# Moving weight loads and old-row loads to other steps in a two-attention kernel

## The chip, the cores and the metric

The kernel runs on one core of one Trainium2 chip. The metric is the device time of one execution in microseconds; lower is better. Most executions of a kernel agree within 0.3%.

The core has five engines that run at the same time and wait for one another through semaphores. TensorE (PE in the profile) multiplies matrices, VectorE (DVE) and ScalarE (ACT) work elementwise and reduce, GpSimd (POOL) does elementwise work too, and SyncE (SP) issues nearly all DMA transfers. Every engine works through its own instructions in order. An instruction that waits therefore holds up all that stands behind it on that engine, SyncE's transfers included.

## The reference, cut to what matters

Two attention layers on separate inputs, each with S = 2048 positions, D = 576 columns and 32 heads of 18 columns; the outputs stand side by side.

- A: every position attends to eight positions, its own and those 2, 4, ... 14 before it.
- B: full attention, every position to all 2048.

```
qkv = x @ wqkv                      # both layers
A:  logits = q . k[pos - 2*i], i = 0..7, masked below 0;  softmax over i;  o = sum of attn * v
B:  p = softmax(q k^T / sqrt(18));  o = p v
out = concat(oA @ woA, oB @ woB)    # [1, 2048, 1152], float32
```

## The kernel before

**Order.** The program is written out by hand, step by step. After the projections there are 512 steps: 8 groups of 4 heads of B, and in each group 4 blocks of 512 queries times 16 tiles of 128 keys. Group g begins at step 64 g, so the last group (7) begins at step 448, and its block b at 448 + 16 b. A step issues four score matmuls (line 269), their four exponentials on ScalarE (line 277), and the products of an earlier step with v into the tile `po` (line 742). Everything else is hung between the steps by an agenda: `plan(start, [(n, f), ...])` puts the function f on step start + n, `later(n, f)` puts it n steps after the present one, and `due()` runs what stands on the present step, in the order in which it was put there. What is planned at the start of the program thus stands ahead of what a `later` adds to the same step. The order within the agenda is the order on SyncE's queue and on GpSimd.

**Maxima of B.** The scores are exponentiated after a maximum per query has been taken out. Beside the scores of the present block, TensorE computes scores once more with queries and keys swapped (line 158) and VectorE reduces them (line 166). When all of a block's maxima are there, `least` (line 176) gathers them, `turn` (183) transposes them a step later, `halve` (101 and 102, on GpSimd) splits them into a high and a low half, and `place` (195) writes these as extra rows into the query tile `qs` by eight small DMAs, two steps later in the last group. The first score matmul of a block (line 269) needs these rows. At some steps `together` runs two steps as one, with half an output product of A (line 1245) between their scores.

**Attention A** is computed on GpSimd and VectorE in eight pieces (`local(j)`), each spread over some 80 steps: `match` (914, 918, 921), the softmax (932, 938, 941, 948, 951), `weighted` (957 to 960), the split (964, 969), then a store to `dao` (972), a load of it by heads (`get`, 987 and 989, tiles `at`, `ahl` and for the last half piece `aq`), and the product with woA (1245).

**Output of B.** `finish` normalises a block: it sends the sums out and back through `drec` (785, 787, 788), multiplies on GpSimd (789), splits (790, 791) and stores to `do` (777, or 780 in the last group). The product with woB runs in the last group. Rows of the heads 0 to 27, called old rows, come back from `do` by `fetch_old(b)` (line 1057): four chunks of 126 rows (seven heads), each as a high and a low tile, thus eight DMAs of 252 KB for each block b. They land for b = 0 in the `qs` of group 6's set, for b = 1 in its `ks`, for b = 2 and 3 in other tiles. The rows of the last four heads come by `stack_new` (1076, 1080).

**Weights of B.** `load_wo` loads woB in five chunks: four of 126 rows, the fifth of four pieces of 18 rows. The landing tile `y` is one of four that rotate, shared with output tiles. The fifth chunk's tile is first filled with zeros on GpSimd (854); then come its four DMAs (857), and six steps later the split (101, 102) into the set that group 5 left. `load_wo_stack(p)`, for p = 0 and 1, loads weights for the last four heads in the same manner (877, two DMAs at 879, split), and nine steps later copies the middle rows from lo to hi by two DMAs (886). Before, each chunk of woB stood two steps behind the last from step 455 on, the fifth at 463, the stacks at 465 and 467.

Of the kernel before, what the change touches and what calls it, by code (L numbers as in the profile page):

```python
# [17 lines left out]
D = 576  # L18
H = 32
DH = 18  # L20
# [12 lines left out]
STEPS = NB * NT  # L33
# [15 lines left out]
def ap(t, *dims):  # L49

    return bass.AP(tensor=t.tensor, offset=t.offset, ap=[list(t.ap[0])] + [list(d) for d in dims])


def rows(t, *dims):

    return bass.AP(tensor=t.tensor, offset=t.offset, ap=[list(d) for d in dims])
# [3 lines left out]
def two_attentions(ctx: ExitStack, tc, xa, wa, woa, xb, wb, wob, out):  # L60
# [6 lines left out]
    load = nc.sync.dma_start  # L67
# [32 lines left out]
    def split_on(engine, hi, lo, raw):  # L100
        engine.tensor_copy(hi, raw)
        engine.tensor_sub(lo, raw, hi)
# [5 lines left out]
    def later(n, f):  # L108
        agenda[step + n].append(f)

    def plan(start, pieces):
        for n, f in pieces:
            agenda[start + n].append(f)
# [194 lines left out]
    def halves(r, odd, w, x, wcols, xcols, weights_move=False):  # L308

        at = slice(64 * r, 64 * r + 64)  # L310
        both = [p for c in range(4) for p in pairs(c, w, x, wcols, xcols)] + pairs(4, w, x, wcols, xcols)[: 1 + (r == odd)]
        return [(b[at], a[at]) if weights_move else (a[at], b[at]) for a, b in both]
# [68 lines left out]
    with (tc.tile_pool(name="x", bufs=1, side="right") as xp,  # L381
# [103 lines left out]
        if True:  # L485
# [9 lines left out]
            chunks = [[(0, 0, 128)], [(0, 128, third - 128), (D, 0, 256 - third)], [(D, 256 - third, 128)]]  # L495
# [185 lines left out]
            for k in range(2, 14):  # L681
                n = 46 if k == 2 else 36 + 4 * k
# [7 lines left out]
            def leave_a(c, b, n, ps):  # L690
                o = xp.tile([128, 512], F32, name="ohi", bufs=4)
                nc.scalar.activation(o[:n], ps, AF.Copy)  # L692
                load(da[128 * c : 128 * c + n, HALO + 512 * b : HALO + 512 * b + 512], o[:n])
# [23 lines left out]
            for c, b in order:  # L717
                n = min(128, 3 * D - 128 * c)
                work_list.append(((b % 2, ws[c][0], xas[b][0], slice(0, n), every),
                                  lambda ps, n=n: ps[:n], lambda ps, c=c, b=b, n=n: leave_a(c, b, n, ps)))  # L720
# [123 lines left out]
    wo = {}  # L844
# [1 line left out]
    producing = set()  # L846
    copied = set()

    def load_wo(k, src, *pieces):

        raw = work.tile([128, D], F32, name="y", bufs=4)
        n = 0
        if len(pieces) == 4:
            nc.gpsimd.memset(raw, 0.0)
            n = 128
        for at, c0, m in pieces:
            load(raw[at : at + m], src[c0 : c0 + m])
            n = max(n, at + m)
        if k == "a":
            hi = work.tile([128, D], F32R, name="wohi", bufs=5)  # L860
            lo = work.tile([128, D], F32R, name="wolo", bufs=5)
        else:

            c = len(wo.get(k, []))
            hi, lo = (ap(t[:, 0, 0, :] if len(t.shape) == 4 else t[:, 0, :], (1, NB * 1024))[:, D * c : D * c + D]
                      for t in sets[(NG - 3) % 3])
        wo.setdefault(k, []).append((hi, lo))
        later(3 if k == "a" else 6, lambda: split_on(nc.gpsimd, hi[:n], lo[:n], raw[:n]))

    wstack = []  # L870
# [1 line left out]
    def load_wo_stack(p):  # L872

        hi, lo = (ap(t[:, 0, 0, :] if len(t.shape) == 4 else t[:, 0, :], (1, NB * 1024))[:, D * (5 + p) : D * (6 + p)]
                  for t in sets[(NG - 3) % 3])
        raw = work.tile([128, D], F32, name="y", bufs=4)
        nc.gpsimd.memset(raw, 0.0)
        for r in range(2):
            load(raw[64 * r : 64 * r + 3 * DH], rows(wob[DH * (H - 4 + r + 2 * p)], (0, 3), (D, DH), (1, D)))
        wstack.append(hi)  # L880
        later(6, lambda: split_on(nc.gpsimd, hi[:118], lo[:118], raw[:118]))

        def middle():
            for r in range(2):
                at = slice(64 * r + DH, 64 * r + 2 * DH)
                load(hi.bitcast(F32)[at], lo.bitcast(F32)[at])

        later(9, middle)


    def local(j):
# [104 lines left out]
            for_two.add(inside[-1])  # L996

        def sums_of_a(h, n, alone=True):
            his, los = zip(*wo["a"])
            w = his[:4], los[:4], his[4], los[4]  # L1000
            cols = slice(288 * h, 288 * h + 288)
            if h == 0:
                st["y"] = ys["a", j, n] = work.tile([128, D], F32, name="y", bufs=4)
            y = st["y"][:, cols]
            both = [halves(r, 0, w, st["x", n], cols, slice(0, 128), True) for r in range(2)]
            if not alone:
                return both, y
            one, two = beside("scores", *both)
            nc.scalar.activation(y, two, AF.Copy)
            behind_scores.append(lambda: nc.vector.tensor_add(y, one, y))  # L1010
# [3 lines left out]
        pieces = [(33, lower), (35, exponents), (39, share), (60, upper), (61, rest), (64, lambda: put(0)), (66, lambda: put(1))]  # L1014
# [5 lines left out]
        pieces = [(at - soon, f) for at, f in pieces]  # L1020
# [14 lines left out]

    olds = defaultdict(list)

    def fetch_old(b):
        for c in range(4):
            h, n = 7 * c, 126  # L1040
            if b < 2:

                t = sets[(NG - 2) % 3][b]
                o = ap(t[:, c, 0] if b == 0 else t[:, c // 2, 1024 * (c % 2) :], (512, 2), (1, 512))
                o = o[:, 0], o[:, 1]

            elif b == 2:
                o = [work.tile([128, D], F32R, name=nm, bufs=5)[:, :512] for nm in ("wohi", "wolo")]
            elif c < 2:
                o = work.tile([128, 2, 512], F32R, name="pr", bufs=2)  # L1050
                o = o[:, 0], o[:, 1]
            else:
                o = ap(work.tile([128, DH, HALO + SUB], F32R, name="akv", bufs=2), (512, 2), (1, 512))
                o = o[:, 0], o[:, 1]
            for i in range(2):
                first = do[i, h // 4, 32 * (h % 4), 512 * b : 512 * b + 512]
                load(o[i].bitcast(F32)[:n], rows(first, (32 * S, 7), (S, DH), (1, 512)))
            olds[b].append([t[:n] for t in o])
# [47 lines left out]
    def beside(kind, *both):  # L1106

        sums_ = [bank(k)[:, :288] for k in (kind, None)]
        turns = [[(sums_[r], *ab, i == 0, i == len(t) - 1) for i, ab in enumerate(t)] for r, t in enumerate(both)]
        pair = kind and sum(given) + 2 <= NG * NB * PIECES * 2  # L1110
        if pair:

            for r in range(2):
                turns[r].insert(6 + 4 * r, None)
        for i in range(max(map(len, turns))):
            for r in range(2):
                if i < len(turns[r]):
                    if turns[r][i]:
                        ps, a, b, start, stop = turns[r][i]
                        nc.tensor.matmul(ps, a, b, start=start, stop=stop)  # L1120
                    else:
                        maximum(r)()
        if pair:

            rings["else"].append(rings["else"].pop(0))
        return sums_
# [72 lines left out]
    for k, src, start, chunks in (  # L1199
        ("a", woa, 28, [[(0, 128 * c, 128)] for c in range(4)] + [[(64 * r, 512, 64) for r in range(2)]]),  # L1200
        ("b", wob, STEPS * (NG - 1) + 7,
         [[(0, 126 * c, 126)] for c in range(4)] + [[(32 * i, 504 + DH * i, DH) for i in range(4)]]),
    ):
        plan(start, [((4 if k == "a" else 2) * c, lambda k=k, src=src, ch=ch: load_wo(k, src, *ch)) for c, ch in enumerate(chunks)])
    for j in range(NJ):
        plan(AT[j], local(j))
    for g in range(1, NG):
        if g > EARLY:
            plan(STEPS * (g - 2) + 1, [(n, f) for n, f in enumerate(stack_loads(g))])
        if g == NG - 1:  # L1210
            plan(STEPS * g, [(4, lambda: fetch_old(0)), (17, lambda: load_wo_stack(0)), (19, lambda: load_wo_stack(1)),
                             (24, lambda: fetch_old(1)), (34, lambda: fetch_old(3)),
                             (38, lambda: fetch_old(2))])
            plan(STEPS * g, [(n, lambda t=t, h=h: partial(t, h)) for n, (t, h) in
                             zip((43, 44, 45, 47, 49, 51), [(t, h) for t in range(3) for h in range(2)])])
            plan(STEPS * g, [(62, lambda: outside.append(lambda: first(3, NB - 1, 0)))])
            for b in range(NB - 1):
                producing.update(STEPS * g + NT * (b + 1) + (23, 15, 7)[b] + n for n in range(8))
        plan(STEPS * (g - 1), [(24, lambda g=g: load_v(g))])
# [52 lines left out]
    while step < ALL:  # L1272
        n, kt = divmod(step, NT)
        g, b = divmod(n, NB)
# [80 lines left out]
```

## Time and profile before

| what | value |
|---|---|
| median of three runs | 1606.92 us (1605.85 to 1607.03) |
| profiled execution | 1605.83 us |
| its span, first to last instruction | 1604.0 us |
| TensorE busy | 1585.2 us, 99% |
| VectorE busy | 1363.6 us, 85% |
| ScalarE busy | 1215.1 us, 76% |
| GpSimd busy | 965.2 us, 60% |
| mean granted clock of TensorE | 0.998 |

The span leaves out what lies before the first and after the last instruction, 1.8 us here. Times in rows of a timeline count from the start of the span. A row of a timeline gives start, length, engine, line, operation, the tile written and the tile read, and in brackets how long the engine was idle before and what ended that. A row of a stretch gives its bounds, its length, the busy time and the number of instructions of each engine, the granted clock, the busy share of the 16 DMA engines, and GB/s. Where rows are merged, "x8" counts instructions. A row of waits gives the engine, the tile and the line that waited, for whom, and then the total, the number and the longest.

### The profile page before, as it was taken

The page shows a single profiled execution, that of the slowest core. Times are in us where ns is not written, and L with a number is a line of the kernel's source. Part 1 is how long each engine was busy: PE and PEld are TensorE (multiplying, and loading weights), DVE is VectorE, ACT ScalarE, POOL GpSimd, SP SyncE. Part 2 cuts the span into 40 slices and gives each one's busy share as a digit, 9 for nine tenths or more (in the row PEclk, how much of TensorE's full clock was granted, in tenths as well). Part 3 has the DMA queues.
Part 4 walks back from the last instruction along what each step waited for, and adds up shares of the span by engine and source line. Part 5 has one row for each costly group of instructions (what it writes and reads, how often), then busy time and mean ns, then how long its engine had stood idle before and what let it go on. Part 6 is the DMA issues. An engine that isn't in the chain of part 4 may idle for free.

```text
span 1604.0 us, 34970 instructions
## 1 busy us (share of the span) xinstructions
PE 1585.2 (99%) x13276; PEld 963.5 (60%) x13276; DVE 1363.6 (85%) x2315; ACT 1215.1 (76%) x2438; POOL 965.2 (60%) x798
## 2 busy tenths in 40 slices
PE   9999999999999999999999999999999999998998
PEld 7999888999543444444445444445445445545676
DVE  5199999999999999999999999999999999896522
ACT  7323441121699999999999999999999999996655
POOL 2305742210266994995896896897896797791000
PEclk9999999999999999999999999999999999999999
DMA  9837954532221362254326335332632231154311
GB/s 264 224 125 196 273 167 130 146 105 80 60 55 50 83 155 67 52 125 96 73 80 146 77 88 119 96 87 54 135 100 66 61 98 36 51 166 153 120 62 60
DMA packets 188025, 175.66 MB, mean 110 GB/s; under 512 B 119416, under 2 KB 133240, under 8 KB 186128
## 3 DMA queue, kind: packets, MB, share of 16 engines
q1 hardware_dynamic: 182992, 161.88, 36.7%
q0 software_dynamic: 4032, 10.63, 3.1%
q8 instruction: 104, 1.70, 0.5%
q10 hardware_dynamic: 832, 0.92, 0.2%
q14 instruction: 65, 0.53, 0.1%
HBM read 98.77 MB, written 73.47 MB: 107 GB/s over the span
## 4 chain that ended last, share of the span: by engine, by line
PE 91%; DVE 3%; DMA 2%; ACT 2%; POOL 1%; issue 1%; SPq 0%; POOLq 0%; DVEq 0%
PE po L742 28%; PE bank L269 18%; PE bank L158 17%; PE bank L364 16%; PE bank L301 5%; PE bank L1120 4%; PE bank L1245 3%; DVE mx L166 3%; ACT e L277 1%; DMA den<-o 1%; DMA rec<-drec 1%; POOL xlo L412 1%; PE bank L516 0%; ACT lg L941 0%; DMA out<-y 0%
## 5 line engine op out<-in xcount | busy, mean ns | idle before, releaser
L166 DVE TENSOR_REDUCE mx<-bank 128x2 f32<-128x512 f32 x2048 | 1279.8, 683 | 132.8 <-PE bank L158 100.2
L277 ACT ACTIVATE e<-bank 128x512 f32<-128x512 f32 x2048 | 1047.5, 607 | 72.6 <-PE bank L269 66.4
L158 PE MATMUL bank<-ks,qs 54*128 54x512 f32 (+1 forms) x2466 | 791.7, 382 | 4.5 <-DVE mx L166 3.0
L158 PEld LDWEIGHTS bank<-ks,qs 54*128 54x128 f32 x2466 | 404.5, 184 | 387.8 <-DVE mx L166 339.4
L269 PE MATMUL bank<-qs,ks 56*128 56x512 f32 x2048 | 597.4, 426 | 6.6 <-DMA qs<-mt 6.6
L742 PE MATMUL po<-e,v 128*19 128x512 f32 x4096 | 531.4, 598 | 0.0
L269 PEld LDWEIGHTS bank<-qs,ks 56*128 56x128 f32 x2048 | 309.7, 185 | 37.8 <-ACT e L277 24.6
L914 POOL TENSOR_TENSOR pr<-aq,akv 128x1024 f32<-128x1024 f32 x72 | 158.4, 2201 | 15.7 <-DMA akv<-da 12.9
L957 POOL TENSOR_TENSOR pr<-lg,akv 128x1024 f32<-128x1024 f32 x72 | 158.4, 2200 | 0.6
L742 PEld LDWEIGHTS po<-e,v 128*19 128x19 f32 x4096 | 73.8, 97 | 138.4 <-issue 132.9
L918 POOL TENSOR_TENSOR pr<-pr 128x1024 f32<-128x1024 f32 x64 | 152.5, 2383 | 5.0
L692 ACT ACTIVATE ohi<-bank 128x512 f32<-128x512 f32 (+1 forms) x56 | 30.4, 595 | 149.2 <-issue 98.5
L364 PE MATMUL bank<-xhi,ahi 64*128 64x512 f32 (+1 forms) x448 | 114.4, 387 | 0.0
L364 PE MATMUL bank<-xhi,alo 64*128 64x512 f32 (+1 forms) x448 | 110.5, 387 | 0.0
L364 PE MATMUL bank<-xlo,ahi 64*128 64x512 f32 (+1 forms) x448 | 107.7, 388 | 0.1
L1245 PE MATMUL bank<-wohi,at 64*128 64x288 f32 x480 | 103.5, 305 | 0.0
L958 POOL TENSOR_TENSOR pr<-pr 128x512 f32<-128x512 f32 x72 | 92.5, 1284 | 5.6
L1245 PEld LDWEIGHTS bank<-wohi,at 64*128 64x128 f32 x480 | 74.7, 184 | 27.6 <-ACT e L277 23.8
L412 POOL TENSOR_TENSOR alo<-raw,ahi 128x512 fp32r<-128x512 f32 (+1 forms) x14 | 17.5, 1253 | 121.0 <-ACT ahi L411 99.4
L504 POOL TENSOR_TENSOR olo<-olo,ohi 128x512 fp32r<-128x512 f32 x36 | 46.0, 1292 | 61.3 <-ACT ohi L503 55.5
L1245 PE MATMUL bank<-wolo,at 64*128 64x288 f32 x240 | 70.0, 292 | 0.0
L364 PEld LDWEIGHTS bank<-xhi,ahi 64*128 64x128 f32 (+1 forms) x448 | 64.6, 182 | 3.5
(202 smaller groups left out, 1793.9 us busy)
## 6 DMA issues: line engine op xcount, KB each, us to landing
do<-n SPq DMA_DIRECT2D x30, 512.0 KB
da<-ohi SPq DMA_DIRECT2D x52, 256.0 KB
akv<-da SPq DMA_DIRECT2D x64, 175.5 KB
out<-y SPq DMA_DIRECT2D x32, 288.0 KB
qs<-dqk SPq DMA_DIRECT2D x30, 288.0 KB
ks<-dqk SPq DMA_DIRECT2D x30, 288.0 KB
at<-dao SPq DMA_DIRECT2D x60, 128.0 KB
rec<-drec SPq DMA_DIRECT2D x29, 256.0 KB
```

The lines of the kernel that those rows point to most:

```text
L158: return nc.tensor.matmul(ps if part is None else ps[:, 256 * r : 256 * r + 256], qs[at, b, p, 128 * t : 128 * t + 128], ks[at, p, 512 * k ...
L166: nc.vector.tensor_reduce(at, ps.rearrange("q (s n) -> q s n", s=2), axis=AX.X, op=ALU.max)
L269: nc.tensor.matmul(ps, ks[at, p, 128 * kt : 128 * kt + 128], qs[at, b, p], start=True, stop=True)
L277: nc.scalar.activation(e, ps, AF.Exp, scale=SCALE)
L301: nc.tensor.matmul(ps, a, b, start=c == i == 0, stop=c == 4 and i == 1)
L364: nc.tensor.matmul(ps, a, b, start=start, stop=stop)
L742: nc.tensor.matmul(po[32 * i : 32 * i + 19], vs[g][:, kt, 19 * i : 19 * i + 19], es[i], start=kt == 0, stop=kt == NT - 1)
L914: nc.gpsimd.tensor_mul(pr, ap(st["q"][:, 2 * c], (SUB, 2), (0, W), (1, SUB)), window(st["k"], c))
L918: nc.gpsimd.tensor_add(st["pr"], st["pr"], pr)
L957: nc.gpsimd.tensor_mul(at, ap(st["lg"], (0, 2), (SUB, W), (1, SUB)), window(st["v"], c))
L958: nc.gpsimd.tensor_add(at[:, :, :4], at[:, :, :4], at[:, :, 4:])
L1245: return nc.tensor.matmul(ps, a, b, start=r == k == 0, stop=r == 1 and k == len(both[1]) - 1)
```

## The change

- The fifth chunk of woB begins at step 421 instead of 463, the stacks at 423 and 425 instead of 465 and 467. All three are thus in group 6.
- Their DMAs are issued three steps after the zero fill instead of right behind it (424, 426 and 428). The split stays six steps after the beginning (427, 429, 431) and the copies of line 886 nine steps after it (432 and 434 instead of 474 and 476).
- Because the fifth chunk now comes ahead of the other four, the chunks of `wo` are kept under their number and no longer as a list in order of loading.
- `fetch_old(1)`, eight DMAs at step 472, becomes two calls of four DMAs: chunks 0 and 1 at step 458, chunks 2 and 3 at step 462.

```diff
-    def load_wo(k, src, *pieces):
+    def load_wo(k, src, c, *pieces):
         raw = work.tile([128, D], F32, name="y", bufs=4)
         n = 0
+        def fetch():
+            for at, c0, m in pieces:
+                load(raw[at : at + m], src[c0 : c0 + m])
         if len(pieces) == 4:
             nc.gpsimd.memset(raw, 0.0)
             n = 128
-        for at, c0, m in pieces:
-            load(raw[at : at + m], src[c0 : c0 + m])
-            n = max(n, at + m)
+            later(3, fetch)
+        else:
+            n = max(at + m for at, c0, m in pieces)
+            fetch()
...
-            c = len(wo.get(k, []))
...
-        wo.setdefault(k, []).append((hi, lo))
+        wo.setdefault(k, {})[c] = hi, lo
...
     def load_wo_stack(p):
...
         nc.gpsimd.memset(raw, 0.0)
+        def fetch(r):
+            load(raw[64 * r : 64 * r + 3 * DH], rows(wob[DH * (H - 4 + r + 2 * p)], (0, 3), (D, DH), (1, D)))
         for r in range(2):
-            load(raw[64 * r : 64 * r + 3 * DH], rows(wob[DH * (H - 4 + r + 2 * p)], (0, 3), (D, DH), (1, D)))
+            later(3, lambda r=r: fetch(r))
...
-    def fetch_old(b):
-        for c in range(4):
+    def fetch_old(b, start=0, end=4):
+        for c in range(start, end):
...
-        plan(start, [((4 if k == "a" else 2) * c, lambda k=k, src=src, ch=ch: load_wo(k, src, *ch)) for c, ch in enumerate(chunks)])
+        plan(start, [((4 if k == "a" else 2) * c if len(ch) < 4 else 421 - start, lambda k=k, src=src, c=c, ch=ch: load_wo(k, src, c, *ch))
+                     for c, ch in enumerate(chunks)])
+    plan(423, [(0, lambda: load_wo_stack(0)), (2, lambda: load_wo_stack(1))])
...
-            plan(STEPS * g, [(4, lambda: fetch_old(0)), (17, lambda: load_wo_stack(0)), (19, lambda: load_wo_stack(1)),
-                             (24, lambda: fetch_old(1)), (34, lambda: fetch_old(3)),
+            plan(STEPS * g, [(4, lambda: fetch_old(0)), (10, lambda: fetch_old(1, 0, 2)), (14, lambda: fetch_old(1, 2, 4)),
+                             (34, lambda: fetch_old(3)),
                              (38, lambda: fetch_old(2))])
```

More of the change, by code (lines that the diff above doesn't have):

```diff
@@ L998, in sums_of_a @@
         def sums_of_a(h, n, alone=True):
-            his, los = zip(*wo["a"])
+            his, los = zip(*(wo["a"][c] for c in range(5)))
             w = his[:4], los[:4], his[4], los[4]
```

## The prediction

> **What bounds the kernel now.** I read the page first (busy time of each engine), then TensorE's list of waits, then stretches of 40 us and of 2 us, then TensorE's and SyncE's timelines around the one wait that is left.
>
> ```profile
> span 1604.0 us, 34970 instructions
> ...
> PE 1585.2 (99%) x13276; PEld 963.5 (60%) x13276; DVE 1363.6 (85%) x2315; ACT 1215.1 (76%) x2438; POOL 965.2 (60%) x798
> ```
>
> TensorE is busy for 1585.2 of 1604.0 us, and the change neither adds, removes nor reorders a matmul. So it can pay, or cost, only in TensorE's waits and in the clock that follows them. From 1270 us to the end its list of waits has one that stands out:
>
> ```profile
> PE bank L269 <- DMA qs<-mt: 6.6, 1, 6.6
> ...
> 1444.00:1484.00 40.00, 33.43 (x294) 21.80 (x292) 27.57 (x48) 25.73 (x52) 5.69 (x7) 0.91 0.43 155
> ...
> 1470.00:1472.00 2.00, 2.00 (x15) 1.95 (x14) 0.90 (x2) 1.49 (x3) 0.00 (x0) 0.50 0.73 250
> ...
> 1474.00:1476.00 2.00, 2.00 (x21) 0.43 (x18) 0.79 (x2) 0.72 (x2) 0.00 (x0) 1.00 0.41 142
> ```
>
> In the rows of stretches the last three columns are granted clock, DMA share and GB/s. The 40 us with the wait hold 33.4 us of matmul, and after the wait the clock is at half speed for some microseconds. What wait and clock cost together is read from one repeated piece of work: two steps with half a product of attention A between them. It begins with a matmul of line 1245 and ends where line 742 begins.
>
> ```profile
> 1455.25 0.40 PE L1245 MATMUL bank<-wohi,at 64*128 64x288 f32 x1
> ...
> 1459.45 1.91 PE L742 MATMUL po<-e,v 128*19 128x512 f32 x16
> 1461.30 0.40 PE L1245 MATMUL bank<-wohi,aq 64*128 64x288 f32 x1
> ...
> 1462.47 0.29 PE L1245 MATMUL bank<-wolo,aq 64*128 64x288 f32 x1
> 1469.33 0.76 PE L269 MATMUL bank<-qs,ks 56*128 56x512 f32 x1 [6.57 <-DMA qs<-mt]
> ...
> 1474.10 1.91 PE L742 MATMUL po<-e,v 128*19 128x512 f32 x16
> ...
> 0.00:1462.80 1462.80, 979.07 (x1918) 1.00 0.42 111
> ```
>
> An undisturbed piece takes 1459.45 - 1455.25 = 4.20 us; this one takes 1474.10 - 1461.30 = 12.80. The excess is 8.6 us: 6.57 of wait and 2.03 of slow clock. The last row counts exponentials of line 277, four to a step: 1918 is two past 4 x 479, so the stall falls inside the pair of steps 479 and 480, at the first scores of step 480 = 448 + 32, block (7, 2). They wait for that block's maxima rows, which place() (line 195) writes into qs.
>
> Why the rows are late stands in SyncE's timeline (start, length, line, DMA, count) and its waits:
>
> ```profile
> 1444.93 6.20 SPq L1057 DMA_DIRECT2D ks<-do  x8
> 1451.24 1.48 SPq L777 DMA_DIRECT2D do<-n  x1
> 1452.77 1.18 SPq L788 DMA_DIRECT2D rec<-drec  x1
> 1454.05 4.77 SPq L886 DMA_DIRECT2D qs<-ks  x4
> 1459.60 6.08 SPq L195 DMA_DIRECT2D qs<-mh  x4
> 1465.78 2.18 SPq L195 DMA_DIRECT2D qs<-mt  x4
> ...
> SPq L195 <- DMA rec<-drec: 2.3, 1, 2.3
> ...
> 1454.86 0.21 POOL L101 CAST mh<-mt 128x32 fp32r<-128x32 f32 x1 [3.29 <-DVE mt L183]
> ...
> 1467.45 1.53 DMA qs<-mt
> ...
> ks<-do SPq DMA_DIRECT2D x8, 252.0 KB
> ```
>
> GpSimd has the rows' high half ready at 1455.07. SyncE is then inside line 886, the four copies of load_wo_stack's middle(), and begins place() only at 1459.60; its first four issues take 6.08 us, because SyncE waits for transfers in flight. Those are the eight old-row loads of block 1 issued from 1444.93 (8 x 252 KB) with the store and the rec load behind them. The chain has the last mt transfer at 1467.45 plus 1.53 us.
>
> **The change part by part.** *Removed around the wait.* Gone from steps 463 to 476 are the loads of the fifth chunk (4 DMAs) and of the two stacks (2 each), the four copies of line 886, and from step 472 the eight ks<-do. At step 474 only the store and the rec load remain; both are then free of the queue that held them. place() would start when GpSimd is ready, at about 1455.1. An undisturbed place is the one of block (7, 1):
>
> ```profile
> 1413.14 0.35 SPq L787 DMA_DIRECT2D drec<-den  x1
> 1416.54 2.36 SPq L195 DMA_DIRECT2D qs<-mh  x4
> 1419.02 2.16 SPq L195 DMA_DIRECT2D qs<-mt  x4
> ...
> 1426.70 0.49 PE L269 MATMUL bank<-qs,ks 56*128 56x512 f32 x1
> ...
> 0.00:1426.90 1426.90, 947.37 (x1856) 1.00 0.42 110
> ```
>
> It issues in 4.64 us (1416.54 to 1421.18). From the end of the last mt issue (1465.78 + 2.18 = 1467.96) to its landing (1468.98) and to TensorE's start (1469.33) were 1.0 and 1.4 us. So the rows are there at 1455.1 + 4.6 + 1.0 to 1.4 = 1460.7 to 1461.1, and TensorE comes at 1462.76 (1469.33 - 6.57): the wait goes to zero with 1.7 us to spare, and the slow clock with it. Ends: a full gain of 8.6; and, if the store and rec still slow the issue by as much as rec did (2.3 us), a wait of 0.6 us and a gain of 8.0. I take 8.6, since their issue no longer follows eight old-row loads.
>
> The Trainium skill's page "TensorE: Matmul & The Clock Gate" (Part 1, the HAM clock gate) says that TensorE falls to half clock after an idle window of about 3.4 us and returns after as much work; this trace agrees: 6.57 us of idle, then 0.50 granted at 1470, 1.00 at 1474. By that rule a leftover wait of 0.6 us would cost no clock.
>
> *Old rows of block 1 in two parts.* Four loads now go out at step 458 and four at 462. The first four stand in the agenda of step 458 ahead of block (7, 1)'s place, since they are planned at the start and place is added later: the same queue, the same neighbour, one block earlier. SyncE has 1413.5 to 1416.5 free for it (drec ends its issue at 1413.49; place waits for GpSimd until 1416.54), and four issues at 6.20 / 8 each are 3.1 us: no delay of the issue, or 0.1. The transfers are 4 x 252 KB = 1.03 MB, and part of what was loaded before is still in flight:
>
> ```profile
> 1413.50:1421.50 8.00, 8.00 (x66) 3.48 (x64) 7.41 (x13) 8.00 (x17) 7.53 (x10) 1.00 0.22 74
> ...
> 1450.00:1452.00 2.00, 2.00 (x24) 1.87 (x21) 2.00 (x4) 2.00 (x4) 1.48 (x2) 1.00 0.45 173
> ```
>
> In the eight microseconds from 1413.5 the trace moves 0.59 MB (74 GB/s). With 1.03 MB more it is 1.62 MB; at the 173 GB/s seen where mostly old rows were moving, that is 9.4 us, done at 1422.9, and mt lands at about 1424, 2.7 us before step 464 (1426.70; the count 1856 = 4 x 464 dates it). Ends: nothing, and 3.7 us if it lands as late after readiness as at step 480 (1468.98 - 1455.07 = 13.9 us; 1416.5 + 13.9 = 1430.4). I take nothing: ahead of it is half of what was ahead there.
>
> The Trainium skill's page "DMA: Bandwidth & Descriptors" (Why a DMA increments its semaphore by 16 and not by 1, on how many engines) says that a DMA runs on the largest count up to 16 that divides the slowest dimension of both sides; seven heads on the DRAM side would give 7 of 16. The DMA share of 0.45 (7.2 of 16) at 1450 agrees. It speaks against the change in one point: splitting the block does not make the old rows faster, and the first half keeps the queue busy for some 6 us (1.03 MB at the row's 173 GB/s), which the sum above already pays.
>
> The second four go out at about 1424.5, behind the first dao store. Behind them are the second dao store and the loads of at and aq for the last products of A, which are pushed back by 1.03 MB and forward by the eight weight loads that have gone, with SyncE's waits on their memsets. The rows are that store, the last of those loads, and the first matmul that takes one:
>
> ```profile
> 1424.06 0.41 SPq L972 DMA_DIRECT2D dao<-aohi  x1
> ...
> 1442.15 0.59 SPq L989 DMA_DIRECT2D aq<-dao  x1
> ...
> 1449.20 0.40 PE L1245 MATMUL bank<-wohi,at 64*128 64x288 f32 x1
> ```
>
> 1.03 MB at 173 GB/s are 6.0 us, the cover is 1449.2 - 1442.7 = 6.5 us, and the first at was issued still earlier: nothing.
>
> *Fifth chunk and stacks at 421 to 434.* GpSimd gets three memsets and three splits there, 3 x 0.58 + 3 x (0.67 + 1.43) = 8.0 us by the rows below, and loses them after 1427:
>
> ```profile
> 1427.83 0.58 POOL L854 MEMSET y<- 128x576 f32 x1
> ...
> 1437.86 0.67 POOL L101 CAST qs<-y 128x576 fp32r<-128x576 f32 x1
> 1438.61 1.43 POOL L102 TENSOR_TENSOR ks<-y,qs 128x576 fp32r<-128x576 f32 x1
> ...
> 1348.94 1.29 POOL L921 TENSOR_TENSOR lg<-pr 128x512 f32<-128x512 f32 x1
> 1355.70 1.29 POOL L938 TENSOR_TENSOR lg<-lg,am 128x512 f32<-128x512 f32 x1 [5.48 <-DVE am L932]
> ...
> 1351.21 0.42 DVE L932 TENSOR_TENSOR am<-lg 128x256 f32<-128x256 f32 x1
> ...
> 1362.51 0.69 ACT L941 ACTIVATE lg<-lg 128x512 f32<-128x512 f32 x1
> ```
>
> Two memsets come ahead of line 921 in program order (steps 421 and 423), so lg ends at 1351.3 instead of 1350.2. VectorE wants it at 1351.21: it would stand 0.1 to 0.3 us. The third memset and two splits, 0.6 + 4.2 us, fill the 5.48 us hole behind line 921; line 938 comes at most 0.5 us later, and ScalarE needs it only at 1362.5. VectorE holds up TensorE's banks when it is late, so I charge 0.2 us, between 0 and 0.5.
>
> The loads there wait on those memsets, so SyncE stands until about 1351.8 at the second stack's. Queued behind it are a rec load and the next at loads; nothing that TensorE takes before step 432. Line 886 moves to 432 and 434, where no maxima rows are due: nothing.
>
> *Sum.* -8.6 + 0.2 = -8.4 us. Against the profiled execution (1605.83 us, span 1604.0) that is 1597.4, span 1595.6. The median of the runs shown, 1606.92, is 1.09 above it: 1598.5.
>
> **Next in line.** After step 480 the old rows of blocks 3 and 2 and the last heads' rows are issued as soon as SyncE is free, so they move forward with TensorE. TensorE's list names no wait there that is set by a transfer.
>
> **The rivals.** (a) *Part of the gain is given back*: rows at step 464, at step 475 or still at 480 land so late that TensorE loses 2 to 5 us. For it: cover of only 2.7 us at 464 and 1.7 us at 480; against: half the bytes ahead. Time 1600.5 to 1603.5. (b) *The change doesn't do what it says*: store, rec load and whatever is delayed from 1424 on still fill the queue at 1451, and place stays as slow. For it: SyncE did wait longest there on the rec load (2.3 us). Against: that load is 256 KB and stood behind 2 MB. Time 1606.9 + 0.2 = 1607.1. (c) *Slower*: the wait goes from step 480 to 464. Were the 1.62 MB to move at the 74 GB/s of 1413.5 to 1421.5, they would take 22 us, mt lands at 1436, TensorE waits 9.3 us and loses 2.03 us of clock: 11.3 - 8.4 = +2.9, time 1609.8. It turns slower from a wait of 6.4 us there (8.4 - 2.03), mt after 1433. Against: 74 GB/s is a queue running empty (share 0.22).
>
> **How the numbers follow.** Forecast 0.70, with its own range 1597.2 to 1600.5 (gain 8.0 to 8.6, VectorE 0 to 0.5, and 1.1 us of scatter: the runs lie between 1605.85 and 1607.03); (a) 0.16; (b) 0.08; (c) 0.06. 0.2% is 3.2 us, about what runs of this kernel can tell from no change: faster is below 1603.7. Faster: 0.70 + 0.15 of (a) = 0.85; same: 0.01 + (b) + 0.01 of (c) = 0.10; slower 0.05. The range 1597.0 to 1604.0 holds the forecast and (a).
>
> **What would show it.** Right: no wait of line 269 on qs<-mt near 1462; granted clock 1.00 all through 1444 to 1484; SyncE at line 195 by 1455.2 with issues of 2.3 and 2.2 us; ks<-do in two groups of four near 1413 and 1424; the hole of 5.48 us ahead of line 938 filled. Wrong: a new wait at 1426.7 (step 464) or at line 1245 near 1449, or the old one kept with a shorter queue ahead of it.

## The result, and the profile after

The changed kernel takes 1605.08 us (median of 22 runs, 1603.06 to 1607.17) against 1606.87 us before (22 runs). The ratio is 0.9989, 95% interval 0.9983 to 0.9996: 1.8 us faster, between 0.6 and 2.7. The prediction was 1598.5 us with a range from 1597.0 to 1604.0.

The profiled execution took 1607.17 us, the longest of the 22; its span is 1605.4 us. It lies 2.8 us behind that of before already at the den load of step 417 (1326.13 instead of 1323.37), ahead of the first step that the change touches (421); why is not known. So absolute times of the two traces differ by about 3 us up to step 470, and only lengths within one trace are compared here.

The wait at step 480 is gone, as predicted, and a new one stands eight steps ahead of it, between steps 471 and 472 (the expectations below call it step 471). The first row of TensorE's waits of the changed kernel from 1270 us on:

```profile
PE bank L158 <- DVE mx L166: 5.6, 3, 5.1
```

and what VectorE waited for, from all engines' waits from 1440 to 1456 us:

```profile
DVE den L786 <- DMA den<-o: 5.2, 1, 5.2
```

The first line 158 matmul of each of the steps 470 to 474, from TensorE's timeline of the changed kernel:

```profile
1442.00 0.38 PE L158 MATMUL bank<-ks,qs 54*128 54x256 f32 x1
...
1444.02 0.38 PE L158 MATMUL bank<-ks,qs 54*128 54x256 f32 x1
...
1451.23 0.58 PE L158 MATMUL bank<-ks,qs 54*128 54x256 f32 x1 [5.08 <-DVE mx L166]
...
1454.86 0.58 PE L158 MATMUL bank<-ks,qs 54*128 54x256 f32 x1
...
1457.42 0.38 PE L158 MATMUL bank<-ks,qs 54*128 54x256 f32 x1
```

and two stretches of it (the last three columns are clock, DMA share, GB/s):

```profile
1452.00:1454.00 2.00, 2.00 (x15) 0.73 (x11) 1.73 (x3) 1.94 (x4) 0.00 (x0) 0.50 0.68 154
...
1458.00:1460.00 2.00, 2.00 (x20) 0.90 (x19) 1.93 (x4) 2.00 (x4) 0.00 (x0) 1.00 0.22 70
```

An undisturbed step takes 1444.02 - 1442.00 = 2.02 us. The three steps from 1444.02 to 1457.42 take 13.40 instead of 6.06: a loss of 7.3 us, 5.1 of wait and 2.2 of slow clock. The old place lost 8.6. The difference, 1.3 us, is most of the measured 1.8.

What VectorE waited for is the den load of block (7, 0), 8 KB, issued by SyncE. SyncE's timeline of the changed kernel:

```profile
1419.51 2.31 SPq L195 DMA_DIRECT2D qs<-mh  x4
1421.93 2.16 SPq L195 DMA_DIRECT2D qs<-mt  x4
1424.13 3.18 SPq L1066 DMA_DIRECT2D ks<-do  x4
1427.35 0.51 SPq L777 DMA_DIRECT2D do<-n  x1
...
1430.60 5.90 SPq L1066 DMA_DIRECT2D ks<-do  x4
1436.74 2.14 SPq L981 DMA_DIRECT2D dao<-ao  x1
1438.99 0.60 SPq L785 DMA_DIRECT2D den<-o  x1
1441.86 3.21 SPq L996 DMA_DIRECT2D at<-dao  x2
...
1465.35 2.29 SPq L195 DMA_DIRECT2D qs<-mh  x4
1467.74 2.15 SPq L195 DMA_DIRECT2D qs<-mt  x4
```

the piece of its chain of waits that is den's way (start, length):

```profile
1438.99 10.70 DMA den<-o
```

and the reciprocal in VectorE's timeline:

```profile
1449.78 0.25 DVE L786 RECIPROCAL den<-den 128x16 f32<-128x16 f32 x1 [5.24 <-DMA den<-o]
```

The same two instructions in the kernel before, in SyncE's and VectorE's timelines:

```profile
1432.85 0.62 SPq L785 DMA_DIRECT2D den<-o  x1
```

```profile
1441.48 0.24 DVE L786 RECIPROCAL den<-den 128x16 f32<-128x16 f32 x1
```

Before, den went out 8.6 us ahead of the reciprocal. The traces also record each count that a transfer adds to its semaphore when it lands; by these counts den landed at 1439.05 then, after 6.2 us, with 2.4 us to spare. Now the second half of the old rows (5.90 us on SyncE for four loads, where the first half took 3.18) and the dao store stand ahead of it. VectorE is ready for the reciprocal at 1449.78 - 5.24 = 1444.54, and den goes out only 5.6 us ahead of that and takes 10.7 us. So it goes out 3.1 us later and is 4.5 us longer on its way; less the 2.4 us of cover, that is the wait of 5.2. By the same counts the old rows ahead of it landed at 1447.95 and the dao store at 1449.44, den at 1449.69.

The 5.90 us are not slower issuing. The four issues by themselves take 3.25 us. The rest is waiting for earlier transfers, mostly the first half of the old rows, as SyncE's waits from 1400 to 1480 us show:

```profile
SPq L1066 <- DMA ks<-do: 2.3, 2, 1.2
```

In these traces eight semaphores take turns among the transfers, and a transfer goes out only when the one eight places ahead of it, which used the same semaphore, has landed: the second, third and fourth load of the second half went out at 1432.52, 1434.75 and 1435.78, each 0.02 us after the last count of its predecessor. So a transfer that is still on its way holds up SyncE eight places later.

The reciprocal is planned on step 470, in VectorE's order ahead of the maxima of the following steps. So VectorE stands for 5.2 us with the reductions behind it, the score banks are not given back, and TensorE stands.

### The profile page after: what moved, and what is told of

Read it like the earlier page. It is cut to its first block, busy times and chain, and to the rows that moved or that the text cites. A ratio compares the mean times of both kernels' runs of the same rounds, so it can differ in the third digit from the quotient of the medians.

```text
span 1605.4 us, 34964 instructions
## 1 busy us (share of the span) xinstructions
PE 1586.9 (99%) x13276; PEld 962.1 (60%) x13276; DVE 1363.3 (85%) x2315; ACT 1214.7 (76%) x2438; POOL 965.1 (60%) x798
## 4 chain that ended last, share of the span: by engine, by line
PE 90%; DVE 4%; DMA 2%; ACT 1%; POOL 1%; issue 0%; SPq 0%; POOLq 0%; DVEq 0%
PE po L742 28%; PE bank L269 18%; PE bank L158 17%; PE bank L364 15%; PE bank L301 5%; PE bank L1256 4%; PE bank L1129 4%; DVE mx L166 3%; DMA den<-o 1%; ACT e L277 1%; POOL xlo L412 1%; DMA dqk<-olo 1%; PE bank L516 0%; DMA more<-xa 0%; DVE as L941 0%
## 5 line engine op out<-in xcount | busy, mean ns | idle before, releaser
L101 POOL CAST mh<-mt 128x32 fp32r<-128x32 f32 x32 | 6.7, 210 | 111.5 <-DVE mt L183 111.5
```

## The experiments

The theory from here on: the change has two parts that work against each other. The early weight loads take away the wait at 480; the early old rows put a new one at 470 to 471, by way of den. The rival: any megabyte that is put ahead of the end of attention A stalls something, so the gain cannot be had. Each comparison is with the kernel before on the same chip.

| run | median us | before us | ratio (95%) | wait of TensorE |
|---|---|---|---|---|
| weights_only | 1600.15 | 1606.65 | 0.9957 (0.9945 to 0.9968) | 480: 0.3 |
| old_only | 1609.75 | 1606.65 | 1.0016 (1.0008 to 1.0025) | 471: 8.9 |
| half_late | 1598.92 | 1606.65 | 0.9953 (0.9941 to 0.9965) | none over 0.6 |
| late_reciprocal | 1599.25 | 1606.65 | 0.9952 (0.9940 to 0.9964) | 480: 0.3 |
| den_on_scalar | 1609.87 | 1607.08 | 1.0016 (1.0007 to 1.0025) | by ScalarE: 8.5 |
| copies_later | 1604.66 | 1607.08 | 0.9985 (0.9976 to 0.9994) | 480: 4.7 |
| loads_early | 1602.50 | 1607.23 | 0.9973 (0.9963 to 0.9984) | 480: 3.0 |

**weights_only: the first part alone.**

```diff
-            (10, lambda: fetch_old(1, 0, 2)), (14, lambda: fetch_old(1, 2, 4)),
+            (24, lambda: fetch_old(1)),
```

> The changed kernel with the old rows of block 1 back at step 472, all eight at once; the weight loads stay early. Theory (the changed kernel lost at step 471 what it won at step 480, because the den load of block (7, 0) sat behind the second half of the old rows): no wait of VectorE for den; at step 480 SyncE reaches line 195 by 1455 instead of 1459.6 (the four copies of line 886, 4.77 us, are gone), its issue still slowed by the eight loads, a wait of 0 to 4 us there; 1599 to 1603 us. Rival (the old rows alone set the wait at 480): it stays at 5 us or more, 1605 to 1607 us.

SyncE's timeline of this run:

```profile
1442.57 6.23 SPq L1066 DMA_DIRECT2D ks<-do  x8
1448.91 0.57 SPq L777 DMA_DIRECT2D do<-n  x1
1449.53 0.66 SPq L788 DMA_DIRECT2D rec<-drec  x1
1455.56 2.28 SPq L195 DMA_DIRECT2D qs<-mh  x4
1457.94 4.23 SPq L195 DMA_DIRECT2D qs<-mt  x4
```

and TensorE's wait at 480:

```profile
PE bank L269 <- DMA qs<-mt: 0.3, 1, 0.3
```

All eight old-row loads stand where they stood before, and the wait is 0.3 us. They are still felt (the mt issue takes 4.23 us instead of 2.15; in SyncE's waits, line 195 stands 2.0 us for the rec load, which went out behind them), but the spare time before step 480 covers all but 0.3 us of that. The second part of the change was not needed for 6.5 us of gain.

**old_only: the second part alone**, in the kernel before.

```diff
-    def fetch_old(b):
-        for c in range(4):
+    def fetch_old(b, start=0, end=4):
+        for c in range(start, end):
...
-            (24, lambda: fetch_old(1)),
+            (10, lambda: fetch_old(1, 0, 2)), (14, lambda: fetch_old(1, 2, 4)),
```

> The kernel before with only the old rows of block 1 moved (458 and 462); the weight loads stay at 463 to 476. Theory: den of block (7, 0) is late by at least as much as in the changed kernel (VectorE waits 5 to 9 us at step 471), and at step 480 a wait of 0 to 2 us is left, since the copies of line 886 still stand ahead of line 195; 1605 to 1610 us. Rival (the early weight loads of group 6 are what costs): no wait at 471, 1598 to 1600 us.

SyncE's timeline of this run:

```profile
1430.55 5.82 SPq L1057 DMA_DIRECT2D ks<-do  x4
1436.54 5.08 SPq L857 DMA_DIRECT2D y<-wob  x4
1442.98 0.36 SPq L972 DMA_DIRECT2D dao<-ao  x1
...
1447.53 0.61 SPq L785 DMA_DIRECT2D den<-o  x1
```

and VectorE's wait:

```profile
DVE den L786 <- DMA den<-o: 9.1, 1, 9.1
```

With the weight loads still between the old rows and den, den goes out at 1447.53 and VectorE waits 9.1 us. At step 480 TensorE does not wait, though the weight loads and the copies of line 886 still stand ahead of line 195; but the stall at 471 has given them 9 us more. Moving the old rows costs more than the wait at 480 that it takes away: 0.16% slower.

**half_late: the second half out of den's way.**

```diff
-            (10, lambda: fetch_old(1, 0, 2)), (14, lambda: fetch_old(1, 2, 4)),
+            (10, lambda: fetch_old(1, 0, 2)), (24, lambda: fetch_old(1, 2, 4)),
```

> The changed kernel with the second half of block 1's old rows at step 472 instead of 462. Theory: den is in time (its load is issued by 1433 and lands within 5 us), and four loads do not delay the maxima rows at 480; no wait over 1 us after 1270 us, 1597 to 1600 us. Rival (whatever 1 MB is put ahead of the end of attention A stalls something): a wait of 3 us or more somewhere between 1440 and 1470, 1602 us or more.

The den load in SyncE's timeline of this run:

```profile
1431.74 0.60 SPq L785 DMA_DIRECT2D den<-o  x1
```

the reciprocal in VectorE's:

```profile
1443.33 0.24 DVE L786 RECIPROCAL den<-den 128x16 f32<-128x16 f32 x1
```

and SyncE's longest wait from 1423 to 1450 us:

```profile
SPq L996 <- DMA dao<-aohi: 9.0, 1, 9.0
```

The reciprocal has no idle time before it, and the gain is 7.7 us. But den did not land within the 5 us that I expected: by its semaphore it landed at 1442.91, 11.2 us after its issue and 0.4 us ahead of the reciprocal. It was in time because it went out early, and only just. The first half still does harm off the path: the loads of at wait 9.0 us for the dao store to land behind it, which is covered.

**late_reciprocal: the den load stays, VectorE comes to it later.** The drec store and the rec load, which follow from the reciprocal, stand three and two steps later too.

```diff
-        times = ... else (1, 6, 7, 10, 13, 14, 15, 16)
+        times = ... else (1, 9, 10, 12, 13, 14, 15, 16)
```

> The changed kernel with no transfer moved, but in the last group VectorE's reciprocal of den three steps later (nine steps behind the block's end instead of six), drec's store ten and the rec load twelve steps behind it. Theory: the wait at step 471 goes, because VectorE then comes to den after it has landed; what is late next are the loads of at, which the changed kernel issued until 1451.1, so at step 475 TensorE waits 0 to 2 us; 1598 to 1601 us. Rival (the load on the queue stalls TensorE anyway, by at): a wait of 4 us or more at step 475, 1603 to 1606 us.

The reciprocal in VectorE's timeline of this run, and the first matmul on at in TensorE's:

```profile
1449.76 0.24 DVE L786 RECIPROCAL den<-den 128x16 f32<-128x16 f32 x1
```

```profile
1451.37 0.40 PE L1256 MATMUL bank<-wohi,at 64*128 64x288 f32 x1
```

The den load is as long on its way as in the changed kernel (issued at 1438.14, landed at 1448.71 by its semaphore, 10.6 us), VectorE takes the reciprocal at the same time (1449.76 here, 1449.78 there), and no wait of TensorE there is over 0.3 us: the place of one small instruction in VectorE's order, with the two transfers that follow from it, decided the loss. The 0 to 2 us that I expected at step 475 for at did not come. The rival falls with this run and half_late.

**den_on_scalar: the den load from another engine.**

```diff
-    lambda: load(den, o[DH:128:32])
+    lambda: (load if g < NG - 1 else nc.scalar.dma_start)(den, o[DH:128:32])
```

> The changed kernel with every transfer at its step, but in the last group the 8 KB den load is issued by ScalarE instead of SyncE. It tells apart two halves of the delay: den was issued at 1438.99 in the changed kernel (six microseconds later than before, SyncE being held at the old rows and the dao store) and landed 10.7 us after that. If the order on SyncE and on its queue is the cause: the load goes out by 1434 and lands in under 5 us, no wait of VectorE for den, TensorE loses at most 2 us at step 475; 1598 to 1601 us. If the transfer engines themselves are taken up by the old rows and the stores, whoever issues: den still lands after 1445, VectorE waits 2 us or more, 1602 to 1605 us.

Neither reading came out: den landed after 1445, as the second had it, but VectorE did not wait for it, and the time is worse than both. (The six microseconds of the expectation compare times of two traces that lie 3 us apart; measured within each trace, as above, it is 3.1.) Two pieces of the chain ("issue" is time in which the engine waited for nothing that the profile shows):

```profile
1431.98 7.51 issue
1439.50 1.14 ACTq L785
```

and TensorE's timeline:

```profile
1440.74 0.58 PE L158 MATMUL bank<-ks,qs 54*128 54x256 f32 x1 [8.49 <-ACTq L249]
```

ScalarE came to the load at 1431.98 and began to issue it at 1439.50. That was not slow issuing but a wait: ahead of the load, ScalarE's instructions for line 785 in this run hold a semaphore wait of 8.9 us, from 1430.5 to 1439.45 (lengths in ns, then the start):

```profile
L785 ACTq EVENT_SEMAPHORE  x1: 8921/8921/8921, 1430.5 to 1430.5; - x1
```

It waits for the semaphore that the den load is to use, and the last transfer on that one was SyncE's first dao store (dao<-aohi, issued at 1427.42): its last count came at 1439.43. SyncE's loads of at, which wait for the same store, go out at 1439.48. So the den load took its turn at a semaphore behind SyncE's transfers although another engine issued it. Now the engine that makes the exponentials was held, and TensorE waited 8.5 us for it. The Trainium skill's page "DMA: Bandwidth & Descriptors" (Issuing engines are not separate DMA queues) says that DMAs from different engines run on the same 16 engines and that issuing from several only saves sequencer time. This run fits that, but is no clean test of it: the load issued by ScalarE still took 8.0 us to land (1439.50 to 1447.45).

**copies_later and loads_early: what made the old wait.** The first, in the kernel before, moves only the four copies of line 886 behind the maxima rows. The second, in weights_only, leaves only these copies where the kernel before had them.

The edit of copies_later (the copies come at steps 480 and 482):

```diff
-        later(9, middle)
+        later(15, middle)
```

The edit of loads_early, beside that of weights_only (the copies come at steps 474 and 476):

```diff
-        later(9, middle)
+        later(51, middle)
```

> The kernel before with one thing moved: the four copies of line 886 fifteen steps behind their stack's start (480 and 482) instead of nine (474 and 476), so behind block (7, 2)'s maxima rows. The loads of the fifth chunk, of the stacks and of block 1's old rows stay where they were. If these copies (4.77 us of SyncE, ahead of line 195) were what made the rows late: line 195 begins by 1455.2, its issue takes 5 to 7 us, a wait of 0 to 2 us at step 480; 1598 to 1601 us. If it was the late start of the eight old-row loads behind the weight loads (1444.93, against 1442.57 where the weight loads were gone): a wait of 3 us or more is left; 1602 to 1606 us.

> The counterpart of copies_later: the fifth chunk and the stacks loaded in group 6 as in the changed kernel, the old rows of block 1 all at step 472, and the four copies of line 886 left at 474 and 476, where the kernel before had them. If the start of the eight old-row loads is the larger part of the wait at step 480 (copies_later still waited 4.7 of 6.6 us there): they start by 1442.6, the copies are issued by 1454 without waiting for GpSimd, and a wait of 0 to 2.5 us is left; 1599 to 1602 us. If the copies are the larger part after all: a wait of 3 us or more, 1603 to 1605 us.

SyncE's timeline in copies_later:

```profile
1446.49 6.26 SPq L1057 DMA_DIRECT2D ks<-do  x8
...
1456.58 4.96 SPq L195 DMA_DIRECT2D qs<-mh  x4
1462.42 5.31 SPq L195 DMA_DIRECT2D qs<-mt  x4
```

TensorE's wait there:

```profile
PE bank L269 <- DMA qs<-mt: 4.7, 1, 4.7
```

SyncE's timeline in loads_early:

```profile
1442.34 6.38 SPq L1066 DMA_DIRECT2D ks<-do  x8
...
1454.21 3.74 SPq L895 DMA_DIRECT2D qs<-ks  x2
1458.73 3.58 SPq L195 DMA_DIRECT2D qs<-mh  x4
```

TensorE's wait there:

```profile
PE bank L269 <- DMA qs<-mt: 3.0, 1, 3.0
```

and two stretches around it:

```profile
1464.00:1468.00 4.00, 2.05 (x16) 2.04 (x18) 0.94 (x2) 1.54 (x3) 1.90 (x3) 0.85 0.46 171
1468.00:1472.00 4.00, 4.00 (x33) 2.54 (x30) 2.52 (x4) 2.34 (x5) 0.00 (x0) 0.73 0.36 121
```

The wait at 480, from one trace each, by what is out of its way: nothing 6.6 us, the copies 4.7, the loads 3.0, both 0.3 (weights_only). So the weight loads were worth 3.6 to 4.4 us of it and the copies 1.9 to 2.7. copies_later came out as its second reading had it. loads_early left 3.0 us where I expected up to 2.5, at the border of both readings, and 1602.5 us where they had up to 1602 and from 1603; the larger part is the loads' all the same. How the loads act is not shown by a run of its own. What the traces show is that without them SyncE is free when den has been turned round, and the old rows start about 2.5 us earlier (1442.34 and 1442.57, against 1444.93 before).

## Why the prediction was wrong

- **The failed step** is the one on the second four loads, "behind the first dao store ... : nothing". I named what stood behind them on SyncE as the second dao store and the loads of at and aq, and checked the cover of at. The den load of step 465 stands there too. I did not ask when it goes out, when VectorE takes it (1441.48 in the trace of before), nor what stands behind that reciprocal on VectorE. The load landed 5.2 us too late, and with the slow clock that cost 7.3 us of the 8.6. The second four loads were also given no time on SyncE. The 3.1 us that I worked out for the first four is right for those (3.18), but the second four held SyncE for 5.90, 2.65 of it waiting for earlier transfers to land.
- **Right, with its size**: the wait at 480 and the clock behind it. In the changed kernel line 195 is issued in 2.29 and 2.15 us (predicted 2.3 and 2.2) and line 269 waits for no transfer. Most of the forecast gain of 8.4 us is there once den is out of the way: half_late and late_reciprocal are 7.7 and 7.4 us faster (ratios 0.9953 and 0.9952, intervals from 0.9940 to 0.9965).
- **Right in effect, half right in cause**: I put the wait at 480 down to the eight old-row loads in flight. weights_only has them at the same step and waits 0.3 us, so they do not make the wait alone: the late weight loads and the copies of line 886 each have a part in it (3.0 and 4.7 us are left when only one of them is out of the way). In old_only, without those eight loads but with all the rest, the wait is gone as well, though there the stall at 471 had lent the queue time. The first part of the change alone earns most of the 8.6 us.
- **Wrong without effect**: the first four loads were to go out ahead of block (7, 1)'s rows. They went out behind them (1424.13 after 1421.93); I had dated VectorE's `least` by TensorE's step, and so `place` one step late. Step 464 did not wait.
- **GpSimd and VectorE at 421 to 434**: GpSimd's hole ahead of the subtraction of the maximum was filled as predicted. Its rows in the changed kernel, line 938 being 947 there:

```profile
1353.85 0.59 POOL L882 MEMSET y<- 128x576 f32 x1
...
1358.87 1.28 POOL L947 TENSOR_TENSOR lg<-lg,am 128x512 f32<-128x512 f32 x1 [0.16 <-DVE am L941]
```

  The 0.2 us charged for VectorE does not show as a wait of TensorE.
- **The rivals**: (a), rows that land late and give back part of the gain, was the right kind, but I priced it at 2 to 5 us and looked for it at 464, 475 and 480 only. (c) had the wait move ahead, but to step 464 and to the maxima rows.
- **The clock rule**: by the Trainium skill's page "TensorE: Matmul & The Clock Gate" (Part 1, the HAM clock gate), an idle window of about 3.4 us slows the clock. In loads_early a wait of 3.0 us already brought it to 0.85 and 0.73 in the two stretches shown above. A wait of 3 us is not free of the clock here.

## What to carry to other kernels

When transfers are moved ahead on an in-order queue, list every transfer that stands behind the new place, the smallest too, and for each the instruction that takes it, and what stands behind that instruction on its own engine. A late 8 KB load cost 7.3 us here. If a load cannot be made earlier, see whether its taker can come later: three steps for one reciprocal gave 7.4 us here. Before a load is moved to another engine, see which semaphore it will wait for. And try the parts of a change one by one: here one part was worth 0.43%, and the other took most of it away.

## What was not expected of the hardware

- The den load on ScalarE went out 7.5 us after ScalarE was free for it, because its semaphore was still in use by a store that SyncE had issued 12 us earlier (den_on_scalar).
- Four old-row loads took 3.18 us on SyncE and, 6.5 us later, 5.90; nearly all of the difference is waiting for the transfers eight places ahead to land.
- An 8 KB load took 10.7 us to land behind them and the dao store, and 3.4 us where no old rows stood ahead of it (weights_only, issued at 1430.33, landed at 1433.72).
- A wait of 3.0 us was enough to slow TensorE's clock (loads_early).
